# A fused attention and two-expert-stage chain on one core: the first batch's instructions put into one order by hand

## The chip, the core and the metric

One Trainium2 chip, one of its cores. The metric is the device time of one execution in microseconds (us), the median of three. TensorE multiplies matrices into PSUM, VectorE and ScalarE work on the results, GpSimd takes some vector work, and SyncE (SP) only issues the loads and stores. Each engine runs its own instructions strictly in the order in which they stand in the program, and waits where an operand isn't there yet.

## The reference

Three stages in a row, for 4 batches of 576 positions and 512 channels, all in float32:

```
scores = where(mask, q @ k.T / 8, -1e9)         # 8 heads of 64; 4 local (band of 32), 4 strided (every 32nd)
x  = softmax(scores) @ v                        # heads side by side: [576, 512]
xk = mu_k * x + (1 - mu_k) * x_prev             # x_prev: x one position earlier; xr likewise
x2 = sigmoid(xr @ w_r) * (relu(xk @ w_k)**2 @ w_v)
out = sum over 4 experts of gate * (causal softmax attention of x2 with wq, wk, wv) @ wo   # the best 2 of 4
```

w_k, w_v and w_r arrive as 64-bit floats and are turned into 32-bit floats on the chip.

## The kernel before

**Stages.** For each batch the sparse attention (`p1_units`) writes x, transposed, into `xT`; the channel mix (`p2_units`) turns it into x2, which is spilled to DRAM; after all four batches the expert attention (`proj_units`, `attn_tiles`) reads it back. The sparse attention of batch b + 1 is mixed into the channel mix of batch b by `interleave`. This case is about the beginning: the sparse attention of batch 0, which has nothing beside it but the weights, and the channel mix of batch 0.

**Sparse attention.** A pair of heads is loaded as one tile `qkv` (queries, keys, values). Its work is cut into stages, 3 for each of two local pairs, 2 for each of two strided pairs, 10 in all. A stage has scores (`sc_f`, TensorE, tiles `sl` and `ss`), masking with the row's maximum (line 208, VectorE, one instruction per group), exp (line 213, ScalarE), the norm (lines 218 to 222, VectorE: add, reciprocal, multiply), a transpose (`tr_f`, tiles `ptl`, `pts`) with its copy out of PSUM (`aT`), and the product with the values (`av_f`, tiles `pol`, `pos`) with its copy into `xT`.

**Weights.** `weight_units` has 20 pieces of 128x512 weights: 4 of w_r, 8 of w_k, 8 of w_v. Of a piece, SP loads the 64-bit words (`wraw`, 512 KB, line 149), ScalarE rescales the two halves of each (lines 154 and 156; "rescale" below), VectorE puts them together in three instructions, each on the result of the one before (lines 158 to 160; "join"), ScalarE rounds the result to the matmul format (line 115, `wkh`, `wvh`; "cast") and VectorE takes the rest (line 118, `wkl`, `wvl`; "low half"). Pieces of w_r in batch 0 need the join alone.

**Channel mix.** A batch is cut in two chunks of columns, A (320) and Z (256). `prep` makes xk and xr of a chunk (lines 412 and 419, `xd`, `xw`, `xf`) and splits xk in two parts (`xh`, `xl`). `mm3` makes the gates (`pr`, in batch 0 in plain float32, line 456), `mm1` the hidden layer (`pk`, 8 groups of 12 matmuls for a chunk, lines 437 to 439; then relu, square and split, lines 441 to 445), `mm2` the output (`pv`, lines 482 to 484). All of `pr`, `pk`, `pv`, `pol` and `pos` share three PSUM banks.

**What sets the order.** The program is written as lists of units; the tile framework's scheduler then sets the final order on each engine by its own estimate of time. `hurry` raises the priority of batch 0's attention and first gates, `behind` holds the attention of batch 1 back until the first half of chunk A's `mm1` has been issued:

```python
    interleave(hurry(A["r"] + A["3"]) + Z["r"] + A["k"] + Z["3"], wk_u[:HK])
    interleave(A["1"][:HK], wk_u[HK:])
    p11 = behind(p11)
    interleave(A["1"][HK:] + Z["k"], wv_u)
    interleave(A["2"] + Z["1"], r_split_units() + p11[:16])
    interleave(Z["2"], p11[16:])
```

Of the kernel before, what the change touches and what calls it, by code (L numbers as in the profile page):

```python
# [16 lines left out]
P = 128  # L17
# [25 lines left out]
def kernel(  # L43
# [98 lines left out]
    def weight_units():  # L142
        units = []

        def piece(dst_h, dst_l, src, whole=False):

            def f():
                raw = p1.tile([P, 1024], I32, tag="wraw", name="wraw", bufs=3)
                nc.sync.dma_start(raw, src.bitcast(I32))
                rv = raw.rearrange("p (n t) -> p n t", t=2)  # L150
                lo, hi = rv[:, :, 0], rv[:, :, 1]
# [4 lines left out]
                nc.scalar.activation(lo, lo.bitcast(U32), AF.Copy, scale=2.0 ** -29)  # L156
                w = p1.tile([P, 512], I32, tag="wf", name="wf", bufs=2)
# [3 lines left out]
                    dst_h if whole else w, hi, -0x80000000, w,  # L161
                    op0=ALU.bitwise_and, op1=ALU.bitwise_or,
                )
                if not whole:
                    split(w.bitcast(F32), dst_h, dst_l, nc.scalar, nc.vector)
            return (1.0, f)

        for kc in range(NKC):
            units.append(piece(wrw[kc].bitcast(I32), None, w_r[:, kc, :], whole=True))
        for hf in range(2):  # L170
            sl = slice(hf * 512, hf * 512 + 512)
            for kc in range(NKC):
                units.append(piece(wkh[:, kc, sl], wkl[:, kc, sl], w_k[:, kc, sl]))
        for fc in range(NFC):
            units.append(piece(wvh[:, fc, :], wvl[:, fc, :], w_v[:, fc, :]))
# [23 lines left out]
    def softmax_group(sc, e, np_, ng, nk, mask_of, tag):  # L199
# [4 lines left out]
        for h in range(nh):  # L204
            for g in range(ng):
# [10 lines left out]
                )  # L216
        s = sm[:np_, :nh * ng]
# [6 lines left out]
    def p1_units(b):  # L224
# [9 lines left out]
        def pair(hp):  # L234
# [3 lines left out]
            def load():  # L238
                src = loc[b, hp] if local else strd[b, hp - NHP // 2]
                t = p1.tile([P, LW], F32, tag="qkv", name=f"qkv{b}_{hp}")  # L240
                kw = S + 32 if local else S
                if b == 0:
# [13 lines left out]
                    st["rest"] = lambda: [nc.sync.dma_start(t[:, cs], src[:, cs]) for cs in more[-1:]]  # L256
                    for cs in more[:-1]:
                        nc.sync.dma_start(t[:, cs], src[:, cs])
# [18 lines left out]
            def local_third(hf):  # L277

                def sc_f():
                    sc = ps_sc(f"sl{b}_{hp}_{hf}")  # L280
                    for g in range(3):
                        i = 3 * hf + g
                        for h in range(2):
# [6 lines left out]
                            )  # L290
                    e = p1.tile([P, 2, 324], F32, tag="e", bufs=3, name=f"el{b}_{hp}_{hf}")
                    e = e.rearrange("p a b -> p (a b)")[:, :3 * LK].unsqueeze(1)
                    softmax_group(
                        [sc], e, P, 3, LK,
# [3 lines left out]
                    st["e", hf] = e  # L298

# [24 lines left out]
                return [(0.9, sc_f), (0.4, tr_f), (0.6, av_f)]  # L324

            def strided_group(gi):
# [3 lines left out]
                def sc_f():  # L330
                    sc = [ps_sc(f"ss{b}_{hp}_{gi}_{h}") for h in range(2)]
                    for g in range(ng):
                        rs = slice(NN * r0 + g * n, NN * r0 + (g + 1) * n)
                        for h in range(2):
# [4 lines left out]
                            )  # L339
                    e = p1.tile([P, 2, 324], F32, tag="e", bufs=3, name=f"es{b}_{hp}_{gi}")  # L340
# [571 lines left out]
```

## Time and profile before

| | |
|---|---|
| three runs | 596.19, 596.63, 596.68 us; median 596.63 |
| profiled execution | 598.2 us, of which 596.3 are the span from the first to the last instruction |
| busy in the span | TensorE 556.5 (93%), VectorE 398.8 (67%), ScalarE 326.8 (55%), GpSimd 104.5 (18%) |
| mean granted TensorE clock | 0.963 of full |
| first `pk` matmul, first `pv` matmul | 80.39 and 97.69 us after the span's start |

Busy time is the time in which an engine has an instruction under way; the idle time before an instruction is put down to what released it last. The granted clock is that of TensorE, 1.00 for 2.4 GHz and 0.50 for 1.2 GHz.

### The profile page before, as it was taken

The numbers are of one execution on the slowest core, as the hardware profiler recorded it, in microseconds if no ns is written. First come the engines' busy times: TensorE is split into PE (matmuls) and PEld (weight loads), VectorE is DVE, ScalarE is ACT, GpSimd is POOL, SyncE is SP. The second block draws the span as 40 slices with busy tenths as digits, with TensorE's granted clock in tenths as the row PEclk, the third lists the DMA queues.
The fourth block names the chain that finished last, engine by engine and source line by source line (L and its number), as shares of the span: only waits on it lengthen the run. The fifth ranks groups of instructions, "written<-read, shape, count | busy, mean of one in ns | idle before, by whom it ended". The sixth has DMA issues, their size and how long they took to land.

```text
span 596.3 us, 12079 instructions
## 1 busy us (share of the span) xinstructions
PE 556.5 (93%) x4408; PEld 504.0 (85%) x4408; DVE 398.8 (67%) x1379; ACT 326.8 (55%) x976; POOL 104.5 (18%) x151
## 2 busy tenths in 40 slices
PE   4657799999999999999999799999999999999987
PEld 4445588998899999989999799999987998898956
DVE  2889887357897455976465982434897883965862
ACT  3898689265254442264360152425786775676763
POOL 0000000000231101320211430054632242211000
PEclk9655999999999999999999899999999999999999
DMA  8566630103401123202112223036341331312112
GB/s 280 172 205 214 198 102 1 46 16 137 171 1 63 35 74 108 91 1 74 57 41 71 72 53 104 5 78 135 71 90 41 76 94 32 76 36 49 45 38 80
DMA packets 27520, 49.71 MB, mean 83 GB/s; under 512 B 3524, under 2 KB 22212, under 8 KB 26692
## 3 DMA queue, kind: packets, MB, share of 16 engines
q1 hardware_dynamic: 22340, 44.21, 22.8%
q0 software_dynamic: 5120, 4.72, 4.5%
q8 instruction: 35, 0.57, 0.4%
q14 instruction: 25, 0.20, 0.1%
HBM read 34.77 MB, written 9.44 MB: 74 GB/s over the span
## 4 chain that ended last, share of the span: by engine, by line
PE 76%; DVE 8%; ACT 7%; DMA 6%; issue 1%; SPq 1%; DVEq 0%; ACTq 0%
PE pv L482 6%; PE pk L437 6%; PE pv L483 6%; PE pv L484 6%; PE pk L438 5%; PE pk L439 5%; PE py L767 4%; PE pt L745 4%; PE sl L285 3%; PE pr L461 2%; DMA wraw<-in_w_v_dram 2%; DMA wraw<-in_w_k_dram 2%; PE s L709 2%; PE pr L462 2%; PE pr L463 2%; PE s L710 2%
## 5 line engine op out<-in xcount | busy, mean ns | idle before, releaser
L437 PE MATMUL pk<-xh,wkh 128*128 128x320 f32 (+1 forms) x256 | 78.5, 308 | 0.1
L482 PE MATMUL pv<-kh,wvh 128*128 128x320 f32 (+1 forms) x256 | 77.0, 305 | 0.0
L438 PE MATMUL pk<-xl,wkh 128*128 128x320 f32 (+1 forms) x256 | 75.5, 295 | 0.0
L483 PE MATMUL pv<-kl,wvh 128*128 128x320 f32 (+1 forms) x256 | 75.2, 296 | 0.0
L439 PE MATMUL pk<-xh,wkl 128*128 128x320 f32 (+1 forms) x256 | 75.2, 294 | 0.0
L484 PE MATMUL pv<-kh,wvl 128*128 128x320 f32 (+1 forms) x256 | 74.7, 294 | 0.0
L441 ACT ACTIVATE rf<-pk 128x320 f32<-128x320 f32 (+1 forms) x64 | 25.5, 406 | 68.9 <-PE pk L439 55.5
L720 ACT ACTIVATE pe<-pe,nm 128x384 f32<-128x384 f32 (+4 forms) x80 | 48.3, 606 | 12.5 <-DVE nm L714 10.2
L437 PEld LDWEIGHTS pk<-xh,wkh 128*128 128x128 f32 x256 | 48.2, 189 | 2.6 <-ACT rf L441 0.3
L482 PEld LDWEIGHTS pv<-kh,wvh 128*128 128x128 f32 x256 | 47.6, 188 | 2.5 <-issue 0.5
L438 PEld LDWEIGHTS pk<-xl,wkh 128*128 128x128 f32 x256 | 48.4, 189 | 0.0
L439 PEld LDWEIGHTS pk<-xh,wkl 128*128 128x128 f32 x256 | 48.3, 189 | 0.0
L483 PEld LDWEIGHTS pv<-kl,wvh 128*128 128x128 f32 x256 | 48.0, 188 | 0.4
L484 PEld LDWEIGHTS pv<-kh,wvl 128*128 128x128 f32 x256 | 47.9, 188 | 0.1
L213 ACT ACTIVATE el<-el,nm 128x96 f32<-128x96 f32 x72 | 26.3, 366 | 36.7 <-DVE nm L208 36.5
L714 DVE CUSTOM_DVE_ANT_0 pe<-s,mcau 128x384 f32<-128x384 f32 (+4 forms) x80 | 36.6, 479 | 10.0 <-PE s L710 9.3
L104 ACT COPY aT<-pt 128x256 f32<-128x256 f32 (+3 forms) x96 | 33.4, 381 | 16.2 <-PE pt L745 15.5
L487 DVE TENSOR_TENSOR sg<-pv,sg 128x320 f32<-128x320 f32 (+1 forms) x32 | 14.6, 457 | 37.9 <-PE pv L484 35.5
L745 PE MATMUL pt<-ident,pe 128*128 128x128 f32 x240 | 37.9, 275 | 2.1 <-ACT aT L104 1.3
L213 ACT ACTIVATE es<-es,nm 108x108 f32<-108x108 f32 (+1 forms) x80 | 30.3, 382 | 13.3 <-DVE nm L208 13.2
L419 DVE SCALAR_TENSOR_TENSOR xf<-xd,mu,xT 128x320 f32<-128x320 f32 (+1 forms) x56 | 33.0, 598 | 4.2 <-POOL xd L412 4.2
L118 DVE TENSOR_TENSOR kl<-rf,kh 128x320 fp32r<-128x320 f32 (+1 forms) x64 | 30.6, 483 | 6.1 <-ACT kh L115 5.0
(150 smaller groups left out, 1572.9 us busy)
## 6 DMA issues: line engine op xcount, KB each, us to landing
qkv<-in_loc_dram SPq DMA_DIRECT2D x6, 1168.0 KB, 5.5
qkv<-in_strd_dram SPq DMA_DIRECT2D x6, 896.0 KB, 4.7
wraw<-in_w_k_dram SPq DMA_DIRECT2D x8, 512.0 KB, 3.6
wraw<-in_w_v_dram SPq DMA_DIRECT2D x8, 512.0 KB, 4.3
x_spill<-sg SPq DMA_DIRECT2D x16, 160.0 KB, 1.9
x2f<-x_spill SPq DMA_DIRECT2D x4, 640.0 KB, 4.6
out_dram<-ot SPq DMA_DIRECT2D x16, 160.0 KB, 1.8
wraw<-in_w_r_dram SPq DMA_DIRECT2D x4, 512.0 KB, 7.5
```

What stands on the lines that cost most here:

```text
L104: nc.scalar.copy(dst, src)
L213: nc.scalar.activation(eg, eg, AF.Exp, bias=nm[:np_, i:i + 1], scale=-1.0, accum_out=sm[:np_, i:i + 1],)
L419: nc.vector.scalar_tensor_tensor(xf[:, :N], d[:, :N], mu[:, which, kc:kc + 1], prv, op0=ALU.mult, op1=ALU.add)
L437: nc.tensor.matmul(pm[:, :N], wkh[:, kc, fs], xh[:, kc, :N], start=(kc == 0), stop=False)
L438: nc.tensor.matmul(pm[:, :N], wkh[:, kc, fs], xl[:, kc, :N], start=False, stop=False)
L439: nc.tensor.matmul(pm[:, :N], wkl[:, kc, fs], xh[:, kc, :N], start=False, stop=(kc == NKC - 1))
L482: nc.tensor.matmul(pm[:, :N], wvh[:, fc, os_], kh[:, :N], start=(fc == 0), stop=False)
L483: nc.tensor.matmul(pm[:, :N], wvh[:, fc, os_], kl[:, :N], start=False, stop=False)
L484: nc.tensor.matmul(pm[:, :N], wvl[:, fc, os_], kh[:, :N], start=False, stop=(fc == NFC - 1))
L714: nc.vector.tensor_tensor_reduce(out=pe[:m, c0:c0 + n], in0=pm[:m, :n], in1=mask, scale=-0.125, scalar=(BIG if i == 0 else nm[:m, 2 * e:2 ...
L720: nc.scalar.activation(pe[:m, :nk], pe[:m, :nk], AF.Exp, bias=last, scale=-1.0, accum_out=sm[:m, e:e + 1],)
L745: nc.tensor.transpose(pt[:, kk * P:(kk + 1) * P], pe[:, c0:c0 + P], ident)
```

## The change

Everything of batch 0 up to the end of chunk A's `mm1` is now written out in one function, `first_batch`, and `pinned` chains its instructions on TensorE, VectorE, ScalarE and SP, each to the one before it on its engine, so that the scheduler can't move them. To make that possible, units are cut into parts: a piece of weights into load, rescale, join and halves; a stage of attention into scores, masking with exp, norm, transpose and product; `prep` of xk into its rounded and its rest part (`kh`, `kl`). In one step i of the loop over the 10 stages, stage i is masked and exponentiated, the halves of an earlier piece, the product of stage i - 3, the transpose of stage i - 2 and the norm of stage i - 1 follow, then a rescale, the join of the piece before, and the scores of stage i + 1. Pieces 0 to 7 (w_r and the first half of w_k) are converted in these steps, the twelve `late` ones (0 to 3 of w_k, 4 to 11 of w_v) behind them, between the gates and in the groups of chunk A's `mm1`.

Other differences: the early `wraw` tiles lie in four buffers that the split hidden layer (`kk`, formerly `kh` and `kl` with eight each) uses later; the third pair's `qkv` tile lies where batch 1's `xT` will be; the second half of a strided stage's transposed weights is copied by VectorE instead of ScalarE; Sigmoid is issued behind chunk A's `mm1`; batch 1's attention and the split of w_r are held behind all of the pinned part, SP's included. No operation of the later batches is changed.

```diff
-        def piece(dst_h, dst_l, src, whole=False):
+        def piece(dst_h, dst_l, src, early=True):
...
+                if early:
+                    raw = p2.tile([P, 1024], I32, tag="kk", name="wraw", bufs=NFC // 2)
+                else:
+                    raw = p1.tile([P, 1024], I32, tag="wraw", name="wraw", bufs=3)
...
-                t = p1.tile([P, LW], F32, tag="qkv", name=f"qkv{b}_{hp}")
+                if b == 0 and hp == 2:
+                    t = p2.tile([P, NKC * (S + 1)], F32, tag="xT", name=f"qkv{b}_{hp}", bufs=2)
+                else:
+                    t = p1.tile([P, LW], F32, tag="qkv", name=f"qkv{b}_{hp}")
...
-                        evac(aT[:n, h, :ng * n], pt[:n, :ng * n], nc.scalar if b == 0 else None)
+                        evac(aT[:n, h, :ng * n], pt[:n, :ng * n], (nc.scalar, nc.vector)[h] if b == 0 else None)
...
+    @contextmanager
+    def pinned():
+        n = len(nc.cur_bb.bb.instructions)
+        yield
+        prev = {}
+        keep = [e.engine for e in (nc.tensor, nc.vector, nc.scalar, nc.sync)]
+        for i in nc.cur_bb.bb.instructions[n:]:
+            if i.engine not in keep:
+                continue
+            if i.engine in prev:
+                tc.add_manual_dep(
+                    i, prev[i.engine].name,
+                    mybir.DependencyInfo(mybir.DependencyClass.NoSync, mybir.DependencyReason.DATA),
+                    reason="pinned",
+                )
+            prev[i.engine] = i
...
+        for i in range(n + 1):
+            if i < n:
+                p10[i][1]()
+            if i - 2 in at:
+                wu[at[i - 2]][3]()
+            if i >= 3:
+                p10[i - 3][4]()
+            if i >= 2:
+                p10[i - 2][3]()
+            if i >= 1:
+                p10[i - 1][2]()
+            if i in at:
+                wu[at[i]][1]()
+            if i - 1 in at:
+                wu[at[i - 1]][2]()
+            if i + 1 < n:
+                p10[i + 1][0]()
...
+        scale(0)
+        p10[n - 2][4]()
+        p10[n - 1][3]()
+        wu[NE - 1][3]()
+        for oc in range(2):
+            A["g"](oc, (0, 1))
+        join(0)
+        scale(1)
+        p10[n - 1][4]()
+        halves(0)
+        A["r"][3][1]()
...
+        halves(1)
+        join(2)
+        scale(3)
+        Z["g"](0, (0, 1, 2, 3))
+        halves(2)
+        join(3)
+        scale(4)
+        Z["g"](1, (0, 1, 2, 3))
...
+        j = 6
+        for fc in range(NFC):
+            join(j)
+            scale(j + 1)
+            A["1"][fc][1]()
+            halves(j)
+            j += 1
+
+        nc.scalar.activation(sg, sg, AF.Sigmoid)
+
+    with pinned():
+        first_batch()
+    main = behind(Z["k"] + A["2"] + Z["1"] + Z["2"])
+    p11 = behind(p11 + r_split_units())
+    k = len(main) - 2 * NKC
+    interleave(main[:k], p11[:20])
+    interleave(main[k:], p11[20:])
```

**VectorE, the pieces of weights beside the gates.** Before (`wf_831`, `wf_841` and `wf_871` are three successive pieces of w_v, named by their joined tile):

```order
L159 ISA wf_831<-wraw_827,wf_831 128x1024
L118 TENSOR_TENSOR wvl_83<-wf_801,wvh_82 128x512
L160 SCALAR_TENSOR_TENSOR wf_831<-wraw_827,wf_831 128x512
L158 TENSOR_SCALAR wf_841<-wraw_837 128x512
L159 ISA wf_841<-wraw_837,wf_841 128x1024
L160 SCALAR_TENSOR_TENSOR wf_841<-wraw_837,wf_841 128x512
L118 TENSOR_TENSOR wvl_83<-wf_831,wvh_82 128x512
L158 TENSOR_SCALAR wf_871<-wraw_867 128x512
L118 TENSOR_TENSOR wvl_83<-wf_841,wvh_82 128x512
```

and now, from the last rest of xk (`xl`) on (`wf_610`, `wf_640` and `wf_656` are late pieces 1, 2 and 3):

```order
L473 TENSOR_TENSOR xl0_0_0_588<-xf0_0_0_3_619,xh0_0_0_587 128x320
L118 TENSOR_TENSOR wkl_76<-wf_610,wkh_75 128x512
L170 TENSOR_SCALAR wf_640<-wraw_287 128x512
L171 ISA wf_640<-wraw_287,wf_640 128x1024
L172 SCALAR_TENSOR_TENSOR wf_640<-wraw_287,wf_640 128x512
L118 TENSOR_TENSOR wkl_76<-wf_640,wkh_75 128x512
L170 TENSOR_SCALAR wf_656<-wraw_562 128x512
L171 ISA wf_656<-wraw_562,wf_656 128x1024
```

The three instructions of a join (lines 170 to 172 now) stood among those of other pieces, with the next pieces' joins ahead of the low half of one; now they stand together, and the low half of each piece stands ahead of the next piece's join. The rows go on like this to the last piece, with one rest of the hidden layer (`kk`) put in ahead of a low half from late piece 6 on.

**ScalarE, the first groups of chunk A's hidden layer.** Before (`wf_871`, `wf_881`: pieces of w_v):

```order
L441 ACTIVATE rf0_0_0_660<-pk0_0_0_647 128x320
L115 CAST wvh_82<-wf_871 128x512
L441 ACTIVATE rf0_0_1_690<-pk0_0_1_677 128x320
L115 CAST wvh_82<-wf_881 128x512
L444 ACTIVATE rf0_0_0_660<-rf0_0_0_660 128x320
L444 ACTIVATE rf0_0_1_690<-rf0_0_1_690 128x320
L115 CAST kh0_0_0_662<-rf0_0_0_660 128x320
L115 CAST kh0_0_1_692<-rf0_0_1_690 128x320
```

and now, from one cast of a w_v piece to the next (`wraw_692` is the piece two further on than `wf_704`; the one of `wf_733` lies between):

```order
L115 CAST wvh_82<-wf_704 128x512
L163 ACTIVATE wraw_692<-wraw_692 128x512
L165 ACTIVATE wraw_692<-wraw_692 128x512
L492 ACTIVATE rf0_0_1_754<-pk0_0_1_741 128x320
L496 ACTIVATE rf0_0_1_754<-rf0_0_1_754 128x320
L115 CAST kk0_0_0_727<-rf0_0_1_754 128x320
L115 CAST wvh_82<-wf_733 128x512
```

The first two groups went side by side, and all 20 rescales stood ahead of the first relu; now the relu, square and cast of one group stand behind a rescale (two instructions) and ahead of the cast of a piece.

**SP's loads.** Before, from the second load on:

```order
L251 DMA qkv0_0_88<-in_loc_dram 128x192
L251 DMA qkv0_0_88<-in_loc_dram 128x224
L258 DMA qkv0_0_88<-in_loc_dram 128x384 x2
L268 DMA ident_61<-in_c_ident_dram 128x128
L256 DMA qkv0_0_88<-in_loc_dram 128x1152
L254 DMA qkv0_1_112<-in_loc_dram 128x1184
L256 DMA qkv0_1_112<-in_loc_dram 128x1152
L272 DMA mstr7_73<-in_c_str_dram 126x126
L272 DMA mstr6_74<-in_c_str_dram 108x108
L273 DMA mu_62<-in_mu_dram 128x8
L149 DMA wraw_94<-in_w_r_dram 128x1024
```

and now:

```order
L274 DMA qkv0_0_88<-in_loc_dram 128x192
L274 DMA qkv0_0_88<-in_loc_dram 128x224
L155 DMA wraw_92<-in_w_r_dram 128x1024
L289 DMA ident_61<-in_c_ident_dram 128x128
L279 DMA qkv0_0_88<-in_loc_dram 128x384 x2
L279 DMA qkv0_0_88<-in_loc_dram 128x1152
L155 DMA wraw_98<-in_w_r_dram 128x1024
L277 DMA qkv0_1_100<-in_loc_dram 128x1184
L155 DMA wraw_102<-in_w_r_dram 128x1024
L279 DMA qkv0_1_100<-in_loc_dram 128x1152
```

The first piece of w_r has moved ahead of the rest of the first pair's queries and keys, the second ahead of the second pair's, the third ahead of that pair's values. Further down, batch 1's first two `qkv` loads, of which one stood ahead of the eight pieces of w_v and the other between them, now stand behind all eight of them.

## Rows read from the trace of the kernel before

**Rows 1.** Stretches from:to: length, busy us (count) by engine, PEclk, DMA share, GB/s.
```profile
...
4.00:12.00 8.00, 4.11 (x39) 3.19 (x39) 3.52 (x26) 3.81 (x19) 0.00 (x0) 1.00 0.95 329
20.00:22.00 2.00, 1.80 (x21) 1.32 (x20) 2.00 (x8) 2.00 (x6) 0.00 (x0) 0.52 0.56 158
30.00:40.00 10.00, 4.53 (x36) 3.31 (x34) 9.38 (x32) 10.00 (x36) 0.00 (x0) 0.50 0.72 220
66.00:68.40 2.40, 0.06 (x1) 0.00 (x0) 2.40 (x7) 1.71 (x3) 0.00 (x0) 1.00 0.91 366
80.40:97.70 17.30, 17.21 (x135) 16.00 (x134) 12.47 (x40) 15.32 (x33) 0.00 (x0) 1.00 0.05 17
97.70:160.70 63.00, 61.71 (x561) 56.27 (x560) 38.52 (x154) 29.33 (x113) 4.10 (x7) 1.00 0.24 87
...
```

**Rows 2.** TensorE in order of time: start, us, line, tiles, shape, count.
```profile
...
56.10 5.92 PE L456 MATMUL pr<-xw,wrw 128*128 128x320 f32 x12
...
80.39 0.49 PE L437 MATMUL pk<-xh,wkh 128*128 128x320 f32 x1
...
88.06 0.71 PE L285 MATMUL sl<-qkv 64*64 64x96 f32 x10
...
97.69 0.31 PE L482 MATMUL pv<-kh,wvh 128*128 128x320 f32 x1
...
```

**Rows 3.** TensorE, line 285 alone, in one stretch: length, busy us (count).
```profile
...
80.40:97.70 17.30, 2.29 (x36) 1.72 (x36) 1.00 0.05 17
...
```

**Rows 4.** VectorE in order of time; the bracket is the idle time before.
```profile
...
5.14 0.26 DVE L208 CUSTOM_DVE_ANT_0 el<-sl,mloc 128x96 f32<-128x96 f32 x1 [5.14 <-PE sl L285]
...
```

**Rows 5.** The same view, two independent neighbours and two dependent ones.
```profile
...
74.00 0.68 DVE L159 CUSTOM_DVE_ANT_0 wf<-wraw,wf 128x1024 uint16<-128x1024 uint16 x1
74.60 0.68 DVE L118 TENSOR_TENSOR wvl<-wf,wvh 128x512 fp32r<-128x512 f32 x1
...
76.25 0.69 DVE L159 CUSTOM_DVE_ANT_0 wf<-wraw,wf 128x1024 uint16<-128x1024 uint16 x1
76.98 0.69 DVE L160 SCALAR_TENSOR_TENSOR wf<-wraw,wf 128x512 int32<-128x512 int32 x1
...
```

**Rows 6.** VectorE by form, 0 to 98 us: busy, mean ns, idle before and releaser.
```profile
...
L159 DVE CUSTOM_DVE_ANT_0 wf<-wraw,wf 128x1024 uint16<-128x1024 uint16 x20 | 13.7, 684 | 0.3
...
L158 DVE TENSOR_SCALAR wf<-wraw 128x512 int32<-128x512 int32 x20 | 8.4, 422 | 0.5 <-ACT wraw L154 0.5
L118 DVE TENSOR_TENSOR wvl<-wf,wvh 128x512 fp32r<-128x512 f32 x8 | 5.5, 687 | 3.7 <-ACT wvh L115 3.7
...
L208 DVE CUSTOM_DVE_ANT_0 el<-sl,mloc 128x96 f32<-128x96 f32 x27 | 5.3, 253 | 9.5 <-PE sl L285 9.5
...
L222 DVE TENSOR_TENSOR el<-el,sm 128x288 f32<-128x288 f32 x6 | 2.7, 454 | 0.1
...
L419 DVE SCALAR_TENSOR_TENSOR xw<-xd,mu,xT 128x320 f32<-128x320 f32 x4 | 2.2, 544 | 0.0
...
L222 DVE TENSOR_TENSOR es<-es,sm 108x648 f32<-108x648 f32 x2 | 1.6, 825 | 0.0
...
L219 DVE RECIPROCAL sm<-sm 128x3 f32<-128x3 f32 x7 | 1.2, 173 | 0.2
...
```

**Rows 7.** ScalarE by form, 0 to 98 us.
```profile
...
L154 ACT ACTIVATE wraw<-wraw 128x512 f32<-128x512 f32 x20 | 13.5, 677 | 12.0 <-DMA wraw<-in_w_v_dram 7.9 <-DMA wraw<-in_w_k_dram 4.0
...
L115 ACT CAST wvh<-wf 128x512 fp32r<-128x512 f32 x8 | 5.0, 620 | 0.5 <-DVE wf L160 0.5
...
L213 ACT ACTIVATE es<-es,nm 126x126 f32<-126x126 f32 x8 | 3.1, 393 | 0.0
...
L441 ACT ACTIVATE rf<-pk 128x320 f32<-128x320 f32 x6 | 2.5, 434 | 1.9 <-DVE kl L118 1.9
...
```

**Rows 8.** DMA issues: KB each, median us from issue to landing.
```profile
...
qkv<-in_loc_dram SPq DMA_DIRECT2D x6, 1168.0 KB, 5.5
...
```

**Rows 9.** TensorE line 461, the gates of the later batches: first and last start.
```profile
...
L461 PE MATMUL pr<-xh,wrh x96: 278/306/469, 155.5 to 356.2; 128*128 128x320 f32 x48, 128*128 128x256 f32 x48
...
```

More of the change, by code (lines that the diff above doesn't have):

```diff
@@ L160, in f, with halves @@
                 nc.vector.scalar_tensor_tensor(
-                    dst_h if whole else w, hi, -0x80000000, w,
+                    dst_h if dst_l is None else w, hi, -0x80000000, w,
                     op0=ALU.bitwise_and, op1=ALU.bitwise_or,
                 )
-                if not whole:
-                    split(w.bitcast(F32), dst_h, dst_l, nc.scalar, nc.vector)
-            return (1.0, f)
+                t["w"] = w.bitcast(F32)
+            def halves():
+                if dst_l is not None:
+                    split(t["w"], dst_h, dst_l, nc.scalar, nc.vector)
+            return load, scale, join, halves
         for kc in range(NKC):
-            units.append(piece(wrw[kc].bitcast(I32), None, w_r[:, kc, :], whole=True))
+            units.append(piece(wrw[kc].bitcast(I32), None, w_r[:, kc, :]))
         for hf in range(2):
@@ L255, in load @@
                         more = [slice(c, src.shape[1])]
-                    st["rest"] = lambda: [nc.sync.dma_start(t[:, cs], src[:, cs]) for cs in more[-1:]]
-                    for cs in more[:-1]:
-                        nc.sync.dma_start(t[:, cs], src[:, cs])
+                    st["rest"] = lambda: [nc.sync.dma_start(t[:, cs], src[:, cs]) for cs in more]
                 else:
@@ L380, in p1_units @@
             pair(hp)
+        if b == 0:
+            return units, loads, [f for _, f in stages]
+        stages = [
+            ((cs, lambda f=f: (f[0](), f[1](), f[2]())), (ct, f[3]), (ca, f[4]))
+            for (cs, ct, ca), f in stages
+        ]
         units += loads[0] + loads[1]
@@ L398, in p2_units, with prep @@
             st = {}
-            def prep(which, kc, ci=ci, s0=s0, N=N, st=st):
+            def prep(which, kc, ci=ci, s0=s0, N=N, st=st, part=None):
                 def f():
+                    if part == 1:
+                        st["low", which, kc]()
+                        return
                     whole = b == 0 and which == 1
@@ L423, in f @@
                     he = nc.scalar if b == 0 else nc.vector
-                    if not whole:
-                        split(xf[:, :N], st["h", which][:, kc, :N], st["l", which][:, kc, :N], he, nc.vector)
+                    if whole:
+                        return
+                    h, l = st["h", which][:, kc, :N], st["l", which][:, kc, :N]
+                    if part is None:
+                        split(xf[:, :N], h, l, he, nc.vector)
+                    else:
+                        nc.scalar.copy(h, xf[:, :N])
+                        st["low", which, kc] = lambda: nc.vector.tensor_tensor(
+                            l, xf[:, :N], h.bitcast(F32), op=ALU.subtract
+                        )
                 return (0.0, f)
             U = {"r": [prep(1, kc) for kc in range(NKC)], "k": [prep(0, kc) for kc in range(NKC)]}
+            U["kh"], U["kl"] = ([prep(0, kc, part=i)[1] for kc in range(NKC)] for i in range(2))
             parts.append(U)
@@ L503, in behind @@
             last[i.engine] = i
[L504 removed]
+        last = [last[e] for e in (nc.tensor.engine, nc.vector.engine, nc.scalar.engine, nc.sync.engine)]
         def wrap(f):
```

157 lines of the change are left out of this document (114 added, 43 removed).

## The prediction

> **What bounds the kernel now.** I read the stretches first. From 80.4 us on TensorE is the bound: it is busy for 17.21 of 17.30 us and then for 61.71 of 63.00 [rows 1]. So the end is set by when that part begins and how densely it runs, and the change can only win or lose in what stands ahead of the first `pv` matmul, at 97.69, and in the gaps after it. Ahead of 80.4 the bound is another: between 30 and 40 us VectorE is busy for 9.38 and ScalarE for 10.00 of 10 us, TensorE for 4.53 at a granted clock of 0.50 [rows 1]. There the attention of batch 0 and the conversion of 20 pieces of weights fill both engines; TensorE gets its first `pk` group at 80.39 [rows 2]. In the 17.3 us from there to the first `pv` it does 8 groups of `pk` and 36 instructions of batch 1's scores, 2.29 us of it [rows 3]; a group is thus (17.3 - 2.3) / 8 = 1.87 us, gaps included.
>
> **What the change does to that.** It moves the conversion of 10 late pieces to the gates and the `pk` groups, which lets `pk` start sooner, but it also makes the order rigid. So I follow VectorE, which has most to do, instruction by instruction, up to the end of `pk`. All its work is in the trace; the order gives what waits.
>
> *Slots.* An instruction that doesn't need the one before starts 0.08 us before that one's end (74.00 to 74.60 for 0.68), one that needs it 0.04 after (76.25 to 76.98 for 0.69) [rows 5]. A join, now three dependent instructions in a row, is 0.42 + 0.04 + 0.69 + 0.04 + 0.60 = 1.8 us; with other work between, as mostly before, it was 1.55. A low half is 0.61 [rows 6].
>
> *VectorE's work up to the low half of late piece 1:* 10 joins 18.0; 6 low halves 3.7; 38 maskings at 0.17, 6.5; 6 local norms at 0.21 + 0.21 + 0.37 and 4 strided ones at 0.42 + 0.75 (the larger form for all), 9.4 [rows 6]; the 4 copies from PSUM that it takes over from ScalarE at 0.35, by ScalarE's 0.43 for a like read of PSUM, 1.4 [rows 7]; for chunk A, with every instruction at the 0.54 of `xw`, 4 pairs `xd`, `xw` 4.2 and 8 of `xf` and `xl` 3.8; 4 shorter pairs for chunk Z, about 3.4 [rows 6]. The last are a little high; I take 50 of the 50.4.
>
> *Its waits there*, from the order: 2.6 for the second stage's scores, whose load now has a 512 KB piece of w_r ahead of it (with the identity 960 KB more at 329 GB/s, 3.0 us [rows 1]; the first pieces land at about 3.9, scores take 1.1). 1.0 for the first piece of w_k, which is about the 6 MB mark of the queue. 5.9 in the three steps with a low half: its cast stands on ScalarE behind the step's four or six exps of 0.39 and takes 0.62 [rows 7], which is 1.7, 2.1 and 2.1 longer than VectorE's own maskings. 2.6 for transposes of strided stages, which stand on TensorE behind another stage's product. 2.9 for late piece 0: its cast stands on ScalarE behind the copy of the tenth stage's product, and this on TensorE behind four gate matmuls of 0.98 (12 instructions in 5.92, two to a matmul, at half clock [rows 2]). Together 15. The bounds are 10, with TensorE at full clock throughout (half of the last two terms and a little of the loads go), and 19, with both loads some 2 us later.
>
> VectorE starts at 5.14 [rows 4], so the low half of late piece 1 ends at 5.1 + 50 + 15 = 70.1 us. By the same steps the last `xw` is there at 69 and four gates of chunk Z follow, so `pk` starts at **about 75 instead of 80.4**.
>
> *From there on.* Each further piece is a loop through two engines: join 0.46 + 0.73 + 0.73, cast 0.62 + 0.04, low half 0.61, **3.2 us**, in which VectorE can't begin the next join, since that stands behind the low half. The square, the cast of `kk` and its rest fit beside it: ScalarE has a rescale (2 x 0.57), relu, square and cast of about 0.45 each and the piece's cast in it, 3.0 us [rows 7]. One `pk` group is let through per loop, as the three banks come free by the relus. The eighth group needs the fifth's relu; this follows the cast of late piece 9 and a rescale. Piece 9 ends 8 loops after piece 1, at 70.1 + 25.6 = 95.7, its cast 0.7 earlier; with rescale and relu that makes 96.5, and the eighth group ends at 96.5 + 1.87 = 98.4. Before, `pv` began at 97.69 with 2.29 us of batch 1's scores already done. **First term: 98.4 + 2.3 - 97.7 = +3.0 us.** So the 5 us by which `pk` starts sooner are spent in its gaps, 23 us for 15 of work.
>
> *After that* TensorE is the bound again. Sigmoid, behind the last `pk` cast, and the rest of the last group end some 8 us into `pv`, which has that long before a bank is needed: nothing. The split of w_r and Z's part of xk follow on VectorE and ScalarE, which were idle for 25 and 34 of the 63 us [rows 1]: nothing. Batch 1's first `qkv` load goes out behind the last piece of w_v, which waits for the join of piece 8 at about 91; at 5.5 us [rows 8] it lands at 97, just ahead of need; 3 us late would cost about 2. Batch 1's attention, held back until now, begins at 98.4 instead of 88.06 [rows 2], and batch 1's gates, which need it, began at 155.5 [rows 9]. If it needed 67.4 us again it would end at 165.8, while TensorE's other work ends at 98.4 + 57.8 + 2.3 - 1.3 = 157.2: a wait of 0 to 8.6 us. I take **second term: +2.0 us**, near the lower end, because that attention hardly waited before (1.3 us idle in 63 [rows 1]): its pace was that of TensorE's order. The later batches run the same work in nearly the same order: nothing.
>
> **Sum.** 3.0 + 2.0 = +5.0 us on the profiled execution's 598.2, so 603.2. That execution is 1.6 above the median of the runs, 596.63; for the runs I predict 596.6 + 5.0 = **601.6 us**. The forecast's own range is 598 to 605: the first term goes by the waits' bounds from -2 to +7, not all at once with the second's.
>
> **Rivals.**
>
> *TensorE's clock falls in the `pk` groups.* Each group of 1.87 us would be followed by a gap of 1.3. The rows point both ways: the clock stood at 1.00 through a stretch of 2.40 us with 0.06 of work, but at 20 to 22 us it fell to 0.52, half of 2.4 GHz, after a stretch with gaps and still 1.80 of 2.00 busy [rows 1]. At half clock a group is 3.7 and outlasts the loop of 3.2; from the fourth group, at about 83.7, five of them end at 102.4, 4.0 later: 605.6. The Trainium skill ("TensorE: Matmul & The Clock Gate", section "A second HAM failure mode: psum-queue depth-cycling") tells of a kernel in which TensorE "micro-idles between MM groups frequently enough" that the clock swings between its two levels. By that rule this rival would be the forecast, 605.6 instead of 601.6; the first of the two rows speaks against it.
>
> *The other side: conversion does not pace `pk`.* If the loop of a piece were no longer than a group, `pk` would run from 75 in one piece: 75 + 15 + 2.3 = 92.3 against 97.7, -5.4, and with the second term 593.2. For it: ScalarE and VectorE had slack in the same stretch before, 2.0 and 4.8 of 17.3 us [rows 1]. Against it: all rescales then stood ahead of the first relu, and now 6 whole pieces lie in the groups. It decides at the loop's length: at 2.6 us instead of 3.2 the gain and the loss cancel.
>
> *No change.* TensorE keeps its full clock from the strided stages on; then the first term falls by some 4 to -1, and with a second term of 0 to 2 the time is 595.6 to 597.6. Against it: the same stages ran at 0.50 before.
>
> **Chances.** Forecast 0.50, clock 0.18, other side 0.19, no change 0.13. A measurement tells about 0.2%, 1.2 us, from no change. Faster are the other side and the edge of the forecast's waits, 0.21; within 1.2 us 0.13; slower 0.66. The range takes in half of the other side and most of the clock's case on top of the forecast's: 592 to 607.
>
> **What would show it.** Right: the first `pk` at 73 to 77 us, then groups of 12 at a distance of about 3.2 us with a gap before each that ScalarE's relu or its PSUM bank ends; VectorE idle 0.7 us ahead of each low half, waiting for ScalarE's cast; the last `pk` group's end at 96 to 101; no scores of batch 1 before it; some 2 us of TensorE's idle time shortly before batch 1's gates. The clock's case shows as a PEclk well under 1 between 75 and 100. Wrong: a `pk` stage of 16 us or less, or a first `pk` ahead of 70, which would mean that VectorE waited less than 10 us before it.

## The result, and the profile after

| | before | after |
|---|---|---|
| median of the runs, us | 596.46 (596.19 to 596.68) | 605.64 (604.50 to 605.83) |
| ratio, 95% interval | | 1.0141 (1.0118 to 1.0164) |
| profiled execution, us | 598.2 | 605.46 |
| its span, us | 596.3 | 603.6 |
| first `pk` matmul | 80.39 | 75.0 |
| first `pv` matmul | 97.69 | 98.86 |
| first gate matmul of batch 1 | 155.5 | 165.1 |

The change costs 9.2 us by the medians and 7.3 by the two spans; the profiled execution of before stood 1.7 above its median, which is most of the difference. The time lies inside the stated range of 592 to 607, 0.6 above the forecast's own 598 to 605 and 4.0 above the point. The stretches of the changed kernel that answer to [rows 1] (length, busy us and count of TensorE's matmuls and weight loads, VectorE, ScalarE, GpSimd, granted clock, DMA share, GB/s):

```profile
75.00:97.20 22.20, 15.96 (x98) 14.19 (x96) 19.19 (x34) 19.12 (x40) 0.00 (x0) 1.00 0.70 231
97.20:149.00 51.80, 51.07 (x483) 46.94 (x483) 35.39 (x143) 34.40 (x108) 1.74 (x3) 1.00 0.19 65
149.00:155.00 6.00, 2.64 (x32) 1.92 (x29) 5.39 (x28) 3.76 (x20) 1.09 (x1) 0.90 0.56 199
155.00:165.10 10.10, 10.10 (x69) 8.85 (x68) 5.78 (x28) 2.69 (x13) 2.84 (x4) 0.55 0.31 109
```

Read them from the top. The `pk` stage is 22.2 us long for 16.0 of TensorE's work, at full clock. Then TensorE is dense for 52 us. Then come 6 us in which it works for 2.6, and behind them 10 us in which it never stops and yet does far less, 69 recorded matmuls; the granted clock is 0.55, so nearly all of the stretch is at 1.2 GHz. From 165.1 on the clock is 1.00 again. TensorE in order of time, the row of line 488 for all `pk` groups first:

```profile
L488 PE MATMUL pk<-xh,wkh x32: 307/309/496, 75.0 to 96.7; 128*128 128x320 f32 x32
...
85.58 0.42 PE L488 MATMUL pk<-xh,wkh 128*128 128x320 f32 x1 [1.27 <-ACT rf L492]
...
97.23 1.70 PE L306 MATMUL sl<-qkv 64*64 64x96 f32 x34
98.86 0.41 PE L543 MATMUL pv<-kk,wvh 128*128 128x320 f32 x1
...
151.79 0.62 PE L383 MATMUL pts<-ident,es 126*126 126x126 f32 x4 [1.56 <-DVE es L241]
153.19 0.65 PE L394 MATMUL pos<-aTs,qkv 126*64 126x126 f32 x8 [0.78 <-DVE aTs L106]
154.86 1.30 PE L383 MATMUL pts<-ident,es 108*108 108x108 f32 x6 [1.01 <-DVE es L241]
156.08 2.50 PE L306 MATMUL sl<-qkv 64*64 64x96 f32 x26
...
165.10 0.31 PE L522 MATMUL pr<-xh,wrh 128*128 128x320 f32 x1
```

The first `pv` follows 34 of the 36 score matmuls that stood ahead of it before [rows 2, 3], and starts 1.2 us later than before. The three waits of 1.56, 0.78 and 1.01 us lie at batch 1's last two strided stages: scores, norm, transposes, product, one stage behind the other, with nothing between. What could have stood there, the last 24 `pv` matmuls of batch 0, comes behind them, at half clock.

**Where the time went**, from these rows: 1.2 us up to the first `pv`; TensorE's idle time from there to the first gate, 0.7 + 3.4 instead of 1.3 [rows 1], +2.8; ten microseconds at 0.55 instead of 1.00, 10.1 x 0.45 = 4.5. That is 8.5 us lost. The first gate comes 9.6 us later, since 26 score matmuls of batch 2 (2.50 us at half clock, 1.25 at full) have moved ahead of the gates as well; 8.5 + 1.25 is 9.75.

Behind the first gate the changed kernel needs 438.5 us and the kernel before 440.8, so 2.3 come back: the 1.25 of moved work, and about 1 that is the balance of smaller losses. The largest of these is in the kernel before: it waits 3.4 us at the gates of the last batch, up to 333.4 us, and its granted clock is 0.91 and 0.75 in the two stretches of 5 us from 330 on. The changed kernel's longest wait from 330 to 345 is 0.6, and its clock 1.00. Of the 9.6 us, 7.3 are left at the end, the difference of the spans.

The four largest waits of TensorE between 60 and 180 us (total, times, longest):

```profile
PE pk L488 <- ACT rf L492: 5.9, 5, 1.4
PE pr L507 <- DVE xw L461: 3.6, 3, 2.0
PE pts L383 <- DVE es L241: 2.6, 2, 1.6
PE pos L394 <- DVE aTs L106: 1.2, 2, 0.8
```

The pace of the `pk` stage is VectorE's loop, as the prediction has it: join (three instructions), a wait of 0.69 for ScalarE's cast, low half, next join, 3.16 us later:

```profile
78.26 0.42 DVE L170 TENSOR_SCALAR wf<-wraw 128x512 int32<-128x512 int32 x1
78.71 0.69 DVE L171 CUSTOM_DVE_ANT_0 wf<-wraw,wf 128x1024 uint16<-128x1024 uint16 x1
79.43 0.69 DVE L172 SCALAR_TENSOR_TENSOR wf<-wraw,wf 128x512 int32<-128x512 int32 x1
80.81 0.69 DVE L118 TENSOR_TENSOR wvl<-wf,wvh 128x512 fp32r<-128x512 f32 x1 [0.69 <-ACT wvh L115]
81.42 0.42 DVE L170 TENSOR_SCALAR wf<-wraw 128x512 int32<-128x512 int32 x1
```

### The profile page after: what moved, and what is told of

It is laid out like the page before. It is cut to its first block, busy times and chain, and to the rows that moved or that the text cites. A ratio compares the mean times of both kernels' runs of the same rounds, so it can differ in the third digit from the quotient of the medians.

```text
span 603.6 us, 12052 instructions
## 1 busy us (share of the span) xinstructions
PE 557.4 (92%) x4408; PEld 502.5 (83%) x4408; DVE 405.7 (67%) x1383; ACT 329.1 (55%) x972; POOL 105.1 (17%) x151
## 4 chain that ended last, share of the span: by engine, by line
PE 69%; DVE 15%; ACT 6%; DMA 5%; issue 2%; POOL 2%; SPq 0%; DVEq 0%; ACTq 0%; POOLq 0%
PE pv L543 6%; PE pv L544 6%; PE pv L545 6%; PE pk L488 5%; PE pk L490 4%; PE pk L489 4%; PE py L957 4%; PE pt L935 4%; PE sl L306 2%; PE s L899 2%; DVE wf L171 2%; PE s L900 2%; PE pos L394 2%; PE pr L522 2%; PE pol L342 2%
## 5 line engine op out<-in xcount | busy, mean ns | idle before, releaser
L543 PE MATMUL pv<-kk,wvh 128*128 128x320 f32 (+1 forms) x256 | 77.5, 308 | 1.3 <-DVE sg L106 1.3
L544 PE MATMUL pv<-kk,wvh 128*128 128x320 f32 (+1 forms) x256 | 75.8, 298 | 0.0
L545 PE MATMUL pv<-kk,wvl 128*128 128x320 f32 (+1 forms) x256 | 75.4, 297 | 0.0
L543 PEld LDWEIGHTS pv<-kk,wvh 128*128 128x128 f32 x256 | 48.4, 191 | 4.0 <-DVE sg L106 1.5
L544 PEld LDWEIGHTS pv<-kk,wvh 128*128 128x128 f32 x256 | 48.6, 190 | 0.6 <-issue 0.4
L545 PEld LDWEIGHTS pv<-kk,wvl 128*128 128x128 f32 x256 | 48.6, 191 | 0.1
L118 DVE TENSOR_TENSOR kk<-rf,kk 128x320 fp32r<-128x320 f32 (+1 forms) x64 | 30.9, 484 | 7.0 <-ACT kk L115 5.8
```

The costliest lines, as they stand in the source:

```text
L543: nc.tensor.matmul(pm[:, :N], wvh[:, fc, os_], kh[:, :N], start=(fc == 0), stop=False)
L544: nc.tensor.matmul(pm[:, :N], wvh[:, fc, os_], kl[:, :N], start=False, stop=False)
L545: nc.tensor.matmul(pm[:, :N], wvl[:, fc, os_], kh[:, :N], start=False, stop=(fc == NFC - 1))
```

## The experiments

Two theories stood at the start. **A:** the loss lies at the end of batch 0, in the gap and the half clock behind it, and is made by the order of batch 1's attention there. **B:** the loss is the conversion loop, and the rest is its echo. Kernels that were measured together share the runs of the kernel before; its median was 596.44 for the first four experiments, 596.65 for the next four, 597.38 for the two after them and 597.88 for the last. So a difference of 1 or 2 us between kernels of different groups is read from their ratios.

**1. The tail's order alone** (`e1`).

```
-    p11 = behind(p11 + r_split_units())
+    p11 = behind(r_split_units() + p11)
```

> The four r_split units ahead of batch 1's attention instead of behind it, so that the second stretch of the interleave is again 24 units of attention against the last eight pv half-groups, as before the change; the pinned block is untouched. Theory A (the loss lies at the end of batch 0: TensorE has nothing between the last strided stages, waits 3.4 us in 149 to 155 us and then runs 155 to 164 at half clock): pv matmuls now stand between these stages, the granted clock in 145 to 165 is 0.95 or more, the first gate of batch 1 comes 4 to 6 us earlier than 165.1, and the time is 599.5 to 602. Theory B (the loss is the conversion loop of 3.17 us under the pk groups, and what comes behind it is only its echo): the last pk group ends at 97 as it did, and the time stays at 605 to 606.

Measured: 606.74 us (601.45 to 608.11), ratio 1.0155 (1.0105 to 1.0205). Three of its four runs took 605.6 to 608.1 and one 601.45, so it can't be told from the change. Theory A misses by the median; the time is near theory B's, but not in B's way. The order came out as wanted, with `pv` matmuls between the strided stages, and the three waits are gone. In their place TensorE waits once for the load of batch 1's last pair, and runs at half clock behind that. The load queue's issue, the wait, and the stretches around it:

```profile
143.25 1.19 SPq L281 DMA_DIRECT2D qkv<-in_strd_dram  x1
```
```profile
148.72 0.71 PE L363 MATMUL ss<-qkv 64*126 64x126 f32 x8 [2.06 <-DMA qkv<-in_strd_dram]
```
```profile
145.00:149.50 4.50, 2.44 (x25) 2.08 (x23) 2.38 (x7) 0.37 (x1) 0.00 (x0) 1.00 0.67 233
149.50:161.00 11.50, 11.50 (x61) 9.40 (x61) 5.54 (x32) 4.29 (x21) 0.74 (x1) 0.57 0.05 9
```

**2. The joins ahead** (`e2`): each piece's low half stands behind the next piece's join, so that VectorE needn't wait for the cast.

```
-            join(j)
-            scale(j + 1)
+            join(j + 1)
+            halves(j)
+            scale(j + 2)
             A["1"][fc][1]()
-            halves(j)
...
```

The loop between the last gates, just ahead, has the same edit.

> In the last gates and in the pk groups the join of the next piece stands ahead of the low half of the piece before it, so that VectorE has work while ScalarE casts the high half. The loop falls from 3.17 us to VectorE's work alone, about 2.5. Theory A: the first pk group starts about 2.5 us earlier, the last ends 5 to 7 us earlier than 97.2 (TensorE was idle 0.4 to 1.4 us at each group there), the gap and the half clock at the end of batch 0 stay in kind, and the time falls by the 5 to 7 alone: 598.5 to 601. Theory B: both go, the gap behind as the echo of the lateness in front, and the time is 593 to 596.5.

Measured: 601.91 us, ratio 1.0095 (1.0071 to 1.0118), 3.7 less than the change. Neither theory has the time. The size of the step was wrong: the loop fell to 2.97 us, not 2.5, and the last `pk` group ended 1.3 us earlier, not 5 to 7. The gap at the end stayed, as theory A has it, 3.59 of 6 us busy from 149 to 155, but the half clock was shorter: 0.65 there and 0.87 from 155 to 165. What bounds the loop now is ScalarE, which has no idle time in it; its row of instructions for one `pk` group, cast to cast (this one from the third experiment, which has the same edit):

```profile
82.43 0.61 ACT L115 CAST wvh<-wf 128x512 fp32r<-128x512 f32 x1
82.95 0.67 ACT L163 ACTIVATE wraw<-wraw 128x512 f32<-128x512 f32 x1
83.53 0.66 ACT L165 ACTIVATE wraw<-wraw 128x512 int32<-128x512 uint32 x1
84.09 0.41 ACT L492 ACTIVATE rf<-pk 128x320 f32<-128x320 f32 x1
84.53 0.47 ACT L496 ACTIVATE rf<-rf 128x320 f32<-128x320 f32 x1
85.03 0.46 ACT L115 CAST kk<-rf 128x320 fp32r<-128x320 f32 x1
85.40 0.62 ACT L115 CAST wvh<-wf 128x512 fp32r<-128x512 f32 x1
```

**3. Both edits** (`e3`).

> The edits of the tail's order and of the joins ahead together. Theory A: the two gains add up, 593 to 596.5, that is the kernel before or slightly better. Theory B: no better than the joins ahead alone.

Measured: 596.26 us, ratio 0.9994 (0.9981 to 1.0007): the whole loss is gone, 9.4 us by two edits of which one alone gave 3.7 and the other nothing. The time is in theory A's range, but the gains don't add up, they need each other, and neither theory says that. What seems to join them is the load of batch 1's last pair. It waits for the buffer of the second pair: it goes out as that pair's last product ends, at 143.2 with the tail's order alone and at 139.0 with both edits, 4.2 us earlier. TensorE hardly waits for it then, and the clock stays up. (In the changed kernel itself it went out at 140.4, as before, and TensorE didn't wait for it; there the waits were for VectorE.)

```profile
139.05 0.33 SPq L281 DMA_DIRECT2D qkv<-in_strd_dram  x1
```
```profile
PE ss L363 <- DMA qkv<-in_strd_dram: 0.2, 1, 0.2
```
```profile
140.00:155.00 15.00, 14.81 (x135) 12.66 (x134) 12.20 (x57) 7.06 (x33) 0.72 (x1) 1.00 0.36 112
155.00:165.00 10.00, 10.00 (x106) 9.07 (x105) 9.39 (x40) 3.16 (x17) 3.86 (x4) 1.00 0.48 193
```

**4. Matmuls that nobody reads, in the gap of the changed kernel** (`e4`).

```
+    for _ in range(12 if b == 1 and hp == 3 and h == 0 else 0):
+        nc.tensor.matmul(pt[:, :256], wkh[:, 0, :P], wkh[:, 0, :256], start=True, stop=True)
```

> The changed kernel with 24 matmuls more that nobody reads (12 of 128x256, some 1.4 us, ahead of the transposes of each of batch 1's last two strided stages, into the same PSUM bank), standing where TensorE waited 1.6 and 1.0 us. Its waits for data end when they did. Theory A, in the form that most of the tail's price is the clock: the granted clock stays at 0.95 or more in 149 to 165, the first gate of batch 1 comes 3.5 to 5 us earlier, and the time is 600.5 to 602.5 although work was added. Rival (the price is the wait itself, and the low clock costs little since the work behind waits for something else): no gain or a loss of up to 1 us, 605 to 606.5.

Measured: 602.69 us, ratio 1.0106 (1.0084 to 1.0128), 2.9 us *less* than the change with 3.4 us of work more. One group of the filler, and the last two stretches of the result (the second ends 0.1 us sooner):

```profile
149.74 1.69 PE L383 MATMUL pts<-wkh 128*128 128x256 f32 x12
```
```profile
149.00:155.00 6.00, 5.53 (x56) 4.78 (x56) 5.48 (x28) 4.12 (x22) 0.72 (x1) 1.00 0.33 98
155.00:165.00 10.00, 8.88 (x82) 7.81 (x80) 7.23 (x26) 1.41 (x6) 2.70 (x4) 1.00 0.54 202
```

The clock stayed at 1.00 and the first gate came at 161.2 instead of 165.1. A wait of 1.12 us for batch 2's first load took a part back. Theory A is right on the clock; the time is 0.2 above its range.

After these four a third theory, **C**: the change makes TensorE wait for 2 us or more in all near the end of batch 0, in one place or another; its clock falls, and that costs more than the wait.

**5. Holding batch 1's attention back, alone** (`e5`): the kernel before, with one line moved.

```
-    p11 = behind(p11)
     interleave(A["1"][HK:] + Z["k"], wv_u)
+    p11 = behind(p11)
```

> The kernel before with one part of the change alone: batch 1's attention is held behind the last pk group and the last converted piece, no longer behind the first half of them; nothing is pinned and the early order is the old one. Theory C (what the runs so far leave: held back, batch 1's two strided loads go out later, since they wait for the buffers of the first two pairs; TensorE then meets a wait of 2 us or more at 145 to 155 us, and its clock goes to half for some 10 us behind it): the load of batch 1's last pair is issued at 142 or later (140.4 before), a window in 145 to 165 shows a granted clock of 0.5 to 0.7, and the time is 600 to 607. Rival (the hold costs nothing by itself, the pinned early block does): first scores of batch 1 at about 98, no wait over 1 us behind, clock 1.00, 595.5 to 598.

Measured: 597.18 us (595.80 to 602.99), ratio 1.0023 (0.9998 to 1.0048). The rival holds as far as this run reaches: the first scores came at 94.06 instead of 88.06, and it cost nothing that can be told, though two of its ten runs took 600.3 and 603.0. It reaches less far than the change: there the first scores came at 97.2, and the load of batch 1's first pair went out at 90.1, here at 48.2, about as before. My expectation of a later load of the last pair was wrong, too: it went out at 138.85, earlier than before (140.41), because the scheduler put the rest of the attention in another order behind the hold. TensorE waited for it once, and the granted clock was 1.00 from there to 165 us:

```profile
PE ss L336 <- DMA qkv<-in_strd_dram: 1.3, 1, 1.3
```

Much later it has the loss that the kernel before has: a wait of 3.5 us up to 331 us, and a granted clock of 0.70 from 330 to 335.

**6. The attention let go earlier** (`e6`): `behind` is called after the fourth `pk` group; the split of w_r stays where it was.

```
             j += 1
+            if fc == 3:
+                early.extend(behind(p11))
...
-    p11 = behind(p11 + r_split_units())
+    p11 = early + behind(r_split_units())
```

> The changed kernel with batch 1's attention let go behind the fourth pk group instead of behind the whole pinned block; r_split stays behind it, and the order of TensorE at the end of batch 0 comes out as in the changed kernel, the two last strided stages back to back and the last 24 pv matmuls behind them. Theory C: first scores of batch 1 stand in the waits of the last pk groups (1.0 to 1.4 us each), which gives at most 3 us; the gap at 149 to 155 and the half clock behind it stay, since the order there is the same: 602 to 605. Rival (lateness alone makes the gap): the gap goes with it and the time is 596 to 599.

Measured: 606.22 us, ratio 1.0169 (1.0141 to 1.0198). It didn't do what it was meant for: the two loads went out at 90 us, but the scheduler put the first scores at 96.8, against 97.2. So it says nothing on lateness. It is a second look at the change's tail order: the same waits (2.1 and 1.2 us in all), a clock of 0.83 and 0.59 in the two stretches.

**7. Let go earlier, with both edits** (`e7`): `e3` with the two lines of `e6` in the loop, and behind it

```
-    p11 = behind(r_split_units() + p11)
+    p11 = behind(r_split_units()) + early
```

> The joins ahead, the tail's order of before and batch 1's attention let go behind the fourth pk group, together. Theory C: clock 1.00 from 75 to 330, no wait over 1 us behind the pk groups, first gate of batch 1 at 151 to 154, and the time is 593 to 596, so 0.1 to 0.6 % under the kernel before. Rival: the early scores of batch 1 take VectorE and ScalarE, which are both busy 2.97 of each 2.97 us of the pk loop there, the pk groups come later by as much, and the time is that of the tail's order with the joins ahead, 596 to 597.

Measured: 597.58 us, ratio 1.0011 (0.9994 to 1.0029). Again the scores hardly moved (first at 95.26); no gain over `e3`.

**8. Filler in the wait of the first experiment** (`e8`).

```
                     sc = [ps_sc(f"ss{b}_{hp}_{gi}_{h}") for h in range(2)]
+                    for _ in range(18 if b == 1 and hp == 3 and gi == 0 else 0):
+                        nc.tensor.matmul(sc[0][:, :256], wkh[:, 0, :P], wkh[:, 0, :256], start=True, stop=True)
```

> The kernel with the tail's order alone, in which TensorE waited 2.1 us at 147 for batch 1's last strided load and ran at half clock until 161, with 18 matmuls more that nobody reads (128x256, 2.1 us in all) ahead of the scores of that pair. Theory C, that the clock is the larger part of the wait's price: granted clock 0.95 or more in 145 to 165, no gate of batch 1 behind 161, 600.5 to 602.5. Rival (the wait's own length and the late load are the price): 606 to 608.

Measured: 601.12 us, ratio 1.0074 (1.0046 to 1.0103). The load was issued at 142.9, as late as in `e1`, and the fill took the place of the wait. Here are the same two stretches as there, and the gates (their line has moved by two):

```profile
145.00:149.50 4.50, 4.44 (x43) 4.21 (x42) 2.29 (x9) 0.37 (x1) 0.00 (x0) 1.00 0.49 188
149.50:161.00 11.50, 11.50 (x99) 9.27 (x98) 8.89 (x43) 5.07 (x23) 0.72 (x1) 1.00 0.25 84
```
```profile
L524 PE MATMUL pr<-xh,wrh x96: 278/307/636, 158.7 to 360.0; 128*128 128x320 f32 x48, 128*128 128x256 f32 x48
```

In 11.5 us without a pause TensorE did 99 recorded matmuls instead of 61. The first gate came at 158.7 instead of 164.0. The time is 5.6 us less by the medians, 4.8 by the ratios and 4.3 by the spans, although this run has a loss at the last batch's gates that `e1` hasn't (a wait of 3.5 us up to 336.2, and 0.51 and 0.81 in the two stretches of 5 us from 335 on). A wait of 2 us had cost some 5 in clock.

**9. Another split of the tail, pinned block untouched** (`e9`).

```
-    p11 = behind(p11 + r_split_units())
+    p11 = behind(r_split_units() + p11)
...
-    interleave(main[:k], p11[:20])
-    interleave(main[k:], p11[20:])
+    interleave(main[:k], p11[:26])
+    interleave(main[k:], p11[26:])
```

Of the 26 units four are the split of w_r, so 22 of the attention stand in the first stretch; the change has 20 there, the first experiment 16.

> The changed kernel with its pinned block untouched, r_split ahead of batch 1's attention, and 22 of that attention's units in place of 20 in the first stretch of the interleave, so that the last strided pair's scores stand behind more of the other matmuls and the last pv matmuls stand between its stages. No work is added or taken away. Theory C (pinned block worth its own lag alone, some 1.7 us; the rest of the loss is a wait at the end of batch 0 and the half clock behind it): last pk group at 97 as before, granted clock 0.95 or more from 75 to 330, no wait over 1.3 us in 100 to 165, first gate of batch 1 at 154 to 158, 597 to 599.5. Rival (the pinned block's lateness costs more than its 1.7 us, by way of the loads): 600 to 606.

Measured: 601.82 us, ratio 1.0077 (1.0063 to 1.0091): the rival's side. No wait between 100 and 165 us is over 0.9 us, but there are three, and 34 score matmuls of batch 2 stand ahead of the gates and in turn wait for their load. Behind these waits the clock falls all the same, so this run doesn't price the block's lateness by itself:

```profile
PE sl L306 <- DMA qkv<-in_loc_dram: 0.9, 1, 0.9
PE pts L383 <- DVE es L241: 0.7, 1, 0.7
PE pos L394 <- DVE aTs L106: 0.5, 1, 0.5
...
155.00:165.00 10.00, 8.37 (x84) 7.63 (x81) 6.22 (x31) 2.69 (x13) 2.27 (x4) 0.83 0.47 164
```

So the order of the tail can be had better by itself than the change has it (ratio 1.0077 instead of 1.0141), but with the last `pk` at 97 no order that was tried came below 601.

**10. Scores in the waits of the `pk` groups** (`e10`): the first load of batch 1 behind the third `pk` group, its first three stages' scores behind the sixth to eighth, on top of `e3`. `ahead` holds that load and the three blocks of scores, which the stages then leave out.

```
             A["1"][fc][1]()
+            if fc in (2, 5, 6, 7):
+                ahead[(2, 5, 6, 7).index(fc)]()
```

> The joins ahead and the tail's order, and in the pinned block the load of batch 1's first pair behind the third pk group and the scores of its first three stages behind the sixth, the seventh and the eighth, into the three banks that scores have. Theory C: these 18 matmuls (1.4 to 1.7 us) stand where TensorE waited 0.9 to 1.0 us before a pk group, the masks and exps of the three stages stay behind the pinned block, the first gate of batch 1 comes 1 to 2 us earlier than with the joins and the tail's order alone (154.1), and the time is 594 to 595.8, under both kernels. Rival (TensorE's order there is not what bounds the stretch up to the gates; VectorE's masks and the loads are): 596 to 597.

Measured: 607.57 us, ratio 1.0172 (1.0150 to 1.0194). I had put the load too late: in the pinned queue it stood behind the last pieces of w_v, each of which waits for a raw buffer, and it went out at 89.24. TensorE then stood at the first scores for 5.0 us; two later waits for such loads, at 162 us and behind it, took 3.0 us together. The granted clock was 0.51 from 95.5 to 101 us, behind the long wait, and 1.00 from there to 110.

**11. The same scores, with the load in its place** (`e11`).

```
         scale(0)
+        ahead[0]()
...
             A["1"][fc][1]()
-            if fc in (2, 5, 6, 7):
-                ahead[(2, 5, 6, 7).index(fc)]()
+            if fc in (2, 3, 4):
+                ahead[fc - 1]()
```

> The scores of batch 1's first three stages in the pinned block again, with the two mistakes of place of the run before mended: the load of that pair now stands ahead of the first late piece's join, where the load queue waits for a raw buffer anyway (about 58 us), and the scores stand behind the third, fourth and fifth pk group. The order of TensorE behind the pinned block comes out as that of the joins ahead with the tail's order, without these 18 matmuls. Theory C: no wait for a load in the pk groups, the 18 matmuls (1.4 to 2.1 us) lie in the waits of 0.9 to 1.0 us there, no wait over 1 us behind, clock 1.00, the first gate of batch 1 at 152 to 153.5, 594 to 595.8. Rival (the stretch up to the gates is bounded by VectorE's masks and the strided pairs' loads): 596 to 597, first gate at 154.

Measured: **594.27 us (593.90 to 595.39), ratio 0.9941 (0.9920 to 0.9962)**, faster than both kernels, as theory C expected. Three blocks of 12 score matmuls stand in the waits (a `pk` group behind one waits 0.32 instead of 0.94), and the first gate comes at 152.97, in `e3` at 154.1 (its line has moved by six):

```profile
80.98 0.71 PE L306 MATMUL sl<-qkv 64*64 64x96 f32 x12
83.68 0.71 PE L306 MATMUL sl<-qkv 64*64 64x96 f32 x12
84.71 0.41 PE L494 MATMUL pk<-xh,wkh 128*128 128x320 f32 x1 [0.32 <-ACT rf L498]
...
93.64 0.42 PE L494 MATMUL pk<-xh,wkh 128*128 128x320 f32 x1 [0.95 <-ACT rf L498]
...
152.97 0.41 PE L528 MATMUL pr<-xh,wrh 128*128 128x320 f32 x1
```

## Why the prediction was right, and where it was not

*The stretch up to `pk`: right.* "About 75 instead of 80.4" was 75.0, in part by errors that cancel. VectorE's waits up to late piece 1 were 12.2 us (predicted 15, bounds 10 to 19), all the rest took 51.3 instead of 50, and the low half was done at 68.8 instead of 70.1. Its waits between 5 and 71 us:

```profile
DVE el L224 <- PE sl L306: 8.9, 2, 5.4
DVE wkl L118 <- ACT wkh L115: 6.2, 4, 1.9
DVE aTs L106 <- PE pts L383: 1.9, 2, 1.5
DVE wf L171 <- ACT aTl L104: 0.6, 1, 0.6
```

Of the 8.9 us, 5.4 are the start, so the second stage's scores took 3.5 (2.6 predicted, and 1.0 for the first w_k piece, which didn't show). Of the 6.2, 5.5 are the three casts behind the exps (5.9), and 0.7 is late piece 0's (2.9). The transposes took 1.9 (2.6), and a wait of 0.6 at an early join had no term. Late piece 0 and the transposes were priced at half clock; TensorE kept 1.00 until 40 us, where it had run at 0.50 before [rows 1], then 0.73 to 50 and 0.93 to 60 us.

*The loop of 3.2 us: right*, 3.16 with the 0.69 of idle time in it, and "the 5 us by which `pk` starts sooner are spent in its gaps" is what happened. The "other side" rival, that conversion does not pace `pk`, falls.

*First term, +3.0: right in kind, too large.* It was +1.2. The last `pk` ended 1.1 us earlier than predicted (97.3 for 98.4), for the 1.3 by which the low half was done sooner, and the scores behind it took 1.6 in one run of 34, not the 2.3 that they had taken in pieces [rows 3].

*Second term, +2.0: the step that failed.* "Its pace was that of TensorE's order" took the attention's stages to be spread as before. The change also moves the split of w_r behind that attention, and the order at the end of batch 0 came out with two strided stages in a row and nothing between. The rows show 7.3 us lost there instead of 2.0: 2.8 of idle time and 4.5 of half clock. (Behind it the kernel before loses about 1 more than the changed one, at the last batch's gates.) I had bounds of 0 to 8.6 for it, and so the stated range held, which was wide enough for the rivals too; but the price of the clock was in none of its rows' terms. The idle time alone, 2.8, is near the 2.0.

*The clock's rival: right on the clock, wrong on the place.* I priced a fall in the `pk` groups. There the granted clock was 1.00, with 5 waits of 1.0 to 1.4 us. It fell at the end of batch 0, behind waits that I counted at their own length alone. That this rival's 605.6 is the measured time is luck: its 4.0 us were to come from groups that ran at full clock. The rule that I cited, of a clock that swings in gaps between groups of matmuls (the Trainium skill, "TensorE: Matmul & The Clock Gate", section "A second HAM failure mode: psum-queue depth-cycling"), did not hold for the `pk` groups here. The same page (section "Why this matters for your kernels") warns of idle gaps between bursts of matmuls in general; the 0.55 behind the three waits of the tail agrees in kind. The gap that it warns of is longer than any of these three, and there the measurement decides.

*What is shown and what is not.* Shown, by filling the same waits with work that nobody reads (`e4`, `e8`): half clock is the larger part of the tail's price, 4 to 5 us. Shown: the loss goes when the order of the tail and the pace of the joins are mended together (`e3`), and not with the tail's order alone (`e1`, `e9`). Holding the attention's scores back to 94 us costs nothing that can be told by itself (`e5`); to 97 us, with its loads held too, wasn't tried alone. Argued only: that the link between the two edits is the issue of the last pair's load, 143.25 against 139.05; no run moved that load alone, and a third buffer for it wasn't tried. Open: how the pinned block by itself would stand if nothing were lost behind it.

## What to carry to other kernels

A wait of TensorE need not be worth its length alone. Before a reordering is costed, look for the places where several short waits or one of 2 us would come close together, and keep independent matmuls in the queue for them. In this kernel the 24 `pv` matmuls that stood just behind the gap took its three waits away (`e1`), but another wait came in their place until the joins were mended too (`e3`). When an order is fixed by hand on every engine, look at the seam where it ends: what the scheduler made of the work behind it was most of the loss here. And where an in-order loop goes through two engines, put the next piece's first step ahead of this piece's last; count the second engine too, since here it became the bound.

## What was not expected of the hardware

- The granted clock fell behind one wait of 2.06 us (`e1`) and behind waits of 1.56, 0.78 and 1.01 us within 6 us (the change), and then stayed at 0.55 to 0.57 for 10 to 11.5 us in which TensorE was busy without a gap. How long it stays down is not fixed: behind a wait of 5.0 us it was 0.51 for only 5.5 us (`e10`). It did not fall in 22 us of `pk` groups with five waits of 1.0 to 1.4 us, one in each 3.2, nor behind one wait of 1.3 (`e5`).
- Work that nobody reads made the kernel faster twice: 3.4 us of it gave 2.9 (`e4`), 2.1 gave 5.6 (`e8`).
- With the new early order TensorE kept its full clock from 12 to 40 us, where it had run at half from 20 us on [rows 1]. What that gave is not shown, and it may be little: six of the runs of the kernel before have a mean granted clock of 0.991 to 0.997 instead of about 0.96, and took 596.4 to 598.5 us, no less than the others.
